# V's weights in five transfers between the first x tiles, later x loads by halves, and one SwiGLU product ahead of two normalisations

## The chip, the cores and the metric

The kernel runs on one core of one Trainium2 chip. The metric is device time in microseconds (us) of one execution, from the runtime's own measurement. A profiled execution gives, beside it, a span (from the first to the last instruction of the program) and a record of each instruction and each DMA transfer.

The engines are named as the profile names them: PE is TensorE (matrix products, with PEld its weight loads), DVE is VectorE, ACT is ScalarE, POOL is GpSimd, and SP is SyncE, which does no arithmetic here and issues the DMA transfers, one after another, in program order.

## The reference

The input x is one sequence of S = 2048 tokens of width D = 640. It is layer-normalised without weights, and the result xn feeds two branches whose outputs are added to x:

```
xn  = (x - mean(x)) / sqrt(var(x) + 1e-5)
out = x + A(xn) + B(xn)

A:  q, k, v = split(xn @ wqkv)                    # 32 heads of 20
    pq, pk  = q @ w_phi[h], k @ w_phi[h]          # per head
    phi(z)  = [softmax(z), softmax(-z)]           # 40 features per head
    kv = phi(pk)^T v ;  z = sum over tokens of phi(pk)
    o  = phi(pq) kv / (phi(pq) z + 1e-6)
    A  = o @ wo
B:  h = silu(xn @ w1) * (xn @ w3)                 # width F = 1536
    B = h @ w2
```

All weights and activations are bfloat16.

## The kernel before, in words

The 2048 tokens are 16 tiles of 128 tokens (t = 0 to 15); four tiles make a quarter of 512 tokens. The engines run the instructions in the order in which the function issues them (the block stands under a manual schedule), each engine and the SP queue in its own order; waits between them come from the data that they share. Eight DMA semaphores are used in turn: before it issues, a transfer also waits for the landing of the transfer eight places ahead of it.

The work falls into three stretches.

1. The start (lines 129 to 658). For each tile, `stats` (line 557) computes mean and variance on DVE (line 190, then 191) and a first 1/sqrt on POOL (lines 199 and 202); `lx` (line 564) refines it and writes the normalised tile in place (line 242, DVE; tiles 12 and 13 on ACT, line 237). `T` (`x_transposed`, line 247) turns the tile into xnT: tiles 0 to 7 by five 128 x 128 transposes on PE (line 262) that ACT copies out of PSUM (line 268), tiles 8 to 15 by a transposing DMA (line 251). `V` (`v_unit`, line 294) is the product of a tile with V's weights, ten matmuls (line 284), copied out by ACT (line 297). A `unit` is one block of 128 of the 1536 columns of SwiGLU for one quarter: ten matmuls into two PSUM banks, gp and up (line 381), and a tanh on ACT (line 389). Its product is issued later, by calling what `unit()` returned (g0 to g4): two instructions on DVE, gs (line 394) and h (line 397), which read gp and up and so free the two banks. There are six banks, used in turn; each `V` takes two as well. `FB` folds w_phi into K's weights (line 365).
2. Lines 661 to 674: for each tile the features of k (POOL normalises them, line 347), the sums kv, and SwiGLU units between them; then wo is loaded (line 673).
3. Lines 678 to 711: for each tile the features of q, the products with kv, and the output product of 34 matmuls (line 499) with the residual.

The loads at the start, all on the SP queue through `ld` (line 108), go in this order: x tiles 0 and 1 (160 KB each), all of V's weights (one transfer of 800 KB, lines 131 and 132), x tiles 2 and 3; then, held back by two one-element copies on ACT that write into their destinations (lines 587 and 590), the second quarter of x (640 KB in one transfer, `ld_x`, line 111), the first third of w1 and w3 (640 KB each), the third quarter of x, and w_phi. The fourth quarter of x reuses the room of the first, so it waits for the transposes of tiles 0 to 3. The x tiles lie in `xin`, a part of reg_h; V's weights, `wv`, lie in reg_w.

The order written out around the fifth unit, g4, is: phi_blocks() (one DVE instruction, line 356), the normalisation and transfer of tile 13, the matmuls of g4 (line 650), the normalisation of tiles 14 and 15 (`lx(14, 2)`), their transposing DMAs, `V(10)`, the product of g4 (line 654), `V(11)`, the loads of the last half of w1 and w3, the transposed load of Q's weights, and then `V(12)` with the first `FB`s.

Of the kernel before, what the change touches and what calls it, by code (L numbers as in the profile page):

```python
# [8 lines left out]
P = 128  # L9
# [3 lines left out]
def kernel(  # L13
# [24 lines left out]
    _, S, D = A_x.shape  # L38
    H, Dh = 32, 20
    F = B_w1.shape[1]  # L40
    NST, NSC, KD, KF = S // P, S // 512, D // P, F // P
# [19 lines left out]
    x2 = A_x[0]  # L61
# [11 lines left out]
    def pair(name):  # L73
# [18 lines left out]
    xin = reg_h[:, 8 * KF * P : 8 * KF * P + 3 * 4 * D].rearrange(  # L92
        "p (b t d) -> p b t d", b=3, t=4
    )
    w_nat = reg_w[:].rearrange("p (w c f) -> p w c f", w=3, c=KD)
    wkT, wqT, wv = w_nat[:, 0], w_nat[:, 1], w_nat[:, 2]
# [11 lines left out]
    def ld(dst, src):  # L108
        nc.sync.dma_start(out=dst, in_=src)

    def ld_x(q):
        ld(
            xin[:, q % 3],
            x2[q * 512 : (q + 1) * 512, :].rearrange("(t p) d -> p t d", p=P),
        )

    def w_of(i):
        return A_wqkv[:, i * D : (i + 1) * D].rearrange("(c p) f -> p c f", p=P)
# [6 lines left out]
    with tc.manual_schedule():  # L125
        def ldT(dst, i):
            nc.sync.dma_start_transpose(out=dst, in_=A_wqkv[:, i * D : (i + 1) * D])

        for t in range(4):
            ld(xin[:, 0, t], x2[t * P : (t + 1) * P, :])  # L130
            if t == 1:
                ld(wv, w_of(2))


        ident = one.tile([P, P], bf, name="ident")
# [68 lines left out]
        def ln_newton(t, n):  # L204


            r = slice(t, t + n)
            eng = nc.vector if t < BY_DMA else nc.gpsimd
            if n == 1:
                eng.tensor_scalar(  # L210
                    out=rstd[:, r], in0=ry[:, r], scalar1=ve[:, r], scalar2=ry[:, r],
                    op0=ALU.mult, op1=ALU.mult,
                )
            else:
                eng.tensor_mul(out=rstd[:, r], in0=ry[:, r], in1=ry[:, r])
                eng.tensor_mul(out=rstd[:, r], in0=rstd[:, r], in1=ve[:, r])
            if t < BY_DMA:
                nc.vector.scalar_tensor_tensor(
                    out=rstd[:, r], in0=rstd[:, r], scalar=-3.0, in1=ry[:, r],
                    op0=ALU.add, op1=ALU.mult,  # L220
                )
            else:
                nc.gpsimd.tensor_scalar(
                    out=rstd[:, r], in0=rstd[:, r], scalar1=-0.5, scalar2=1.5,
                    op0=ALU.mult, op1=ALU.add,
                )
                nc.gpsimd.tensor_mul(out=rstd[:, r], in0=rstd[:, r], in1=ry[:, r])
            if t in BY_ACT:
                nc.gpsimd.tensor_scalar(
                    out=shift[:, r], in0=mv[:, r, 0], scalar1=rstd[:, r], scalar2=-1.0,  # L230
                    op0=ALU.mult, op1=ALU.mult,
                )

        def ln_x(t):
            xt = xin[:, (t // 4) % 3, t % 4, :]
            if t in BY_ACT:
                nc.scalar.activation(
                    out=xt, in_=xt, func=AF.Identity,
                    scale=rstd[:, t : t + 1], bias=shift[:, t : t + 1],
                )  # L240
                return
            nc.vector.tensor_scalar(  # L242
                out=xt, in0=xt, scalar1=mv[:, t, 0:1], scalar2=rstd[:, t : t + 1],
                op0=ALU.subtract, op1=ALU.mult,
            )
# [130 lines left out]
        def glu_unit(sc, fi):  # L376

            gp, up = bank("gp"), bank("up")
            for ps, w in ((gp, w1), (up, w3)):
                for c in range(KD):  # L380
                    nc.tensor.matmul(  # L381
                        ps[:],
                        w[:, c, fi * P : (fi + 1) * P],
                        xnT[:, c, sc * 512 : (sc + 1) * 512],
                        start=(c == 0),
                        stop=(c == KD - 1),
                    )
            th = work.tile([P, 512], f32, name="th")
            nc.scalar.activation(out=th[:], in_=gp[:], func=AF.Tanh, scale=0.5)  # L389
            return lambda: glu_product(sc, fi, gp, up, th)  # L390
# [143 lines left out]
        def norm_unit(w, g, i):  # L534
            sq = work.tile([P, KD, 160], bf, name="sq")
            nc.scalar.activation(
                out=sq[:], in_=w[:, :, i * 160 : (i + 1) * 160],
                func=AF.Square, accum_out=norms[:, 4 * g + i : 4 * g + i + 1],
            )
# [24 lines left out]
        def lx(t0, n):  # L564
            if t0 < BY_DMA:
                ln_newton(t0, n)
            for t in range(t0, t0 + n):
                ln_x(t)
# [13 lines left out]
        def unit():  # L582
            return glu_unit(*glu.pop(0))


        stats(0, 1)
        nc.scalar.copy(out=xin[0:1, 1, 0, 0:1], in_=ry[0:1, 0:1])
        ld_x(1)
        stats(1, 1)
        nc.scalar.copy(out=w1[0:1, 0, 0:1], in_=ry[0:1, 1:2])  # L590
        ld_glu(0, 512)
        ld_x(2)
        ld(wps[:], A_w_phi.rearrange("h j f -> (h j) f").rearrange("(c p) f -> p c f", p=P))
        lx(0, 1)
# [10 lines left out]
        lx(3, 1)  # L605
        T(3)
        ld_x(3)
        ldT(wkT, 1)
        ld_glu(512, 768)
# [38 lines left out]
        lx(13, 1)  # L648
        T(13)
        g4 = unit()  # L650
        lx(14, 2)
        T(14, 15)
        V(10)
        g4()
        V(11)
        ld_glu(768, F)
        ldT(wqT, 0)
# [4 lines left out]
        for t in range(NST):  # L662
# [7 lines left out]
            fill(1)  # L670
            if t >= 12:
                norm_unit(wkphi, 0, t - 12)
        for k0, k1 in ((0, 3), (3, KD)):
            ld(wo[:, k0:k1], A_wo[k0 * P : k1 * P, :].rearrange("(c p) d -> p c d", p=P))


# [37 lines left out]
    with tc.If(ok == 0):  # L714
# [16 lines left out]
        with tc.For_i(0, NST, 1) as t:  # L731
# [5 lines left out]
            h = hT[:, bass.ds(t, 1)].rearrange("p a f s -> p (a f) s")  # L737
# [30 lines left out]
```

## Time and profile before

| | |
|---|---|
| median of three runs | 274.9 us (274.19 to 274.9) |
| the profiled execution's own time | 274.14 us |
| its span | 272.3 us |
| PE busy | 264.5 us (97% of the span) |
| DVE busy | 190.4 us (70%) |
| ACT busy | 111.8 us (41%) |
| POOL busy | 96.5 us (35%) |
| granted TensorE clock | 1.0 throughout |

The span leaves out 1.8 us of the execution's own time. The busy time of PE includes 60 matmuls on an identity matrix near the start whose results are not used (line 169), and the ends of matmuls are modelled, so that overlapping records can show as longer than the pace at which they follow each other. A few matmul records are missing: a group of five may show as four. In a timeline row the numbers are the start and the length in microseconds, the engine, the line, the operation, what it writes and reads, how many instructions were merged, and in brackets the idle time before the first and what ended it. For SPq rows the length is the time in which the queue issued, not the transfer.

### The profile page before, as it was taken

The page shows a single profiled execution, that of the slowest core. Times are in us where ns is not written, and L with a number is a line of the kernel's source. Part 1 is how long each engine was busy: PE and PEld are TensorE (multiplying, and loading weights), DVE is VectorE, ACT ScalarE, POOL GpSimd, SP SyncE. Part 2 cuts the span into 40 slices and gives each one's busy share as a digit, 9 for nine tenths or more (in the row PEclk, how much of TensorE's full clock was granted, in tenths as well). Part 3 has the DMA queues.
Part 4 walks back from the last instruction along what each step waited for, and adds up shares of the span by engine and source line. Part 5 has one row for each costly group of instructions (what it writes and reads, how often), then busy time and mean ns, then how long its engine had stood idle before and what let it go on. Part 6 is the DMA issues. An engine that isn't in the chain of part 4 may idle for free.

```text
span 272.3 us, 5207 instructions
## 1 busy us (share of the span) xinstructions
PE 264.5 (97%) x2000; PEld 167.8 (62%) x2018; DVE 190.4 (70%) x354; ACT 111.8 (41%) x262; POOL 96.5 (35%) x98
## 2 busy tenths in 40 slices
PE   7799999999999999999999999999999999999995
PEld 7557567555555555555554555677777777777773
DVE  5799850887766677777778778877776677777341
ACT  6656558543555554346555454522222222222000
POOL 5235730354433333344443312333333434433000
PEclk9999999999999999999999999999999999999999
DMA  7995459900000000000000974346665686556641
GB/s 206 337 256 147 79 94 314 218 0 2 0 0 2 0 2 0 1 4 0 0 2 0 278 119 77 77 112 133 144 141 130 130 129 144 127 130 148 145 103 54
DMA packets 60092, 27.14 MB, mean 100 GB/s; under 512 B 47136, under 2 KB 60064, under 8 KB 60064
## 3 DMA queue, kind: packets, MB, share of 16 engines
q1 hardware_dynamic: 60064, 26.77, 42.6%
q8 instruction: 17, 0.28, 0.4%
q14 instruction: 11, 0.09, 0.1%
HBM read 12.81 MB, written 2.62 MB: 57 GB/s over the span
## 4 chain that ended last, share of the span: by engine, by line
PE 90%; DVE 3%; DMA 2%; POOL 2%; issue 1%; SPq 0%; ACT 0%; DVEq 0%
PE acc L499 27%; PE up L381 18%; PE gp L381 18%; PE pq L284 8%; PE pk L284 8%; PE pv L284 5%; DMA reg_h<-in_A_x_dram 2%; PE pkv L407 2%; PE pr L436 2%; PE pf L365 1%; DVE st L190 1%; DVE reg_h L242 1%; POOL ry L202 1%; PE pst L262 1%; DVE reg_h L397 1%
## 5 line engine op out<-in xcount | busy, mean ns | idle before, releaser
L347 POOL TENSOR_TENSOR phi<-phi,rk 128x1320 bf16<-128x1320 bf16 x32 | 77.2, 2414 | 137.5 <-DVE rk L346 125.8
L344 DVE TENSOR_REDUCE sk<-phi 128x66 f32<-128x1320 bf16 x32 | 48.9, 1528 | 41.8 <-ACT phi L311 40.9
L381 PEld LDWEIGHTS <-w 128*128 128x128 bf16 x480 | 45.5, 98 | 50.2
L381 PE MATMUL up<-xnT,w 128*128 128x512 bf16 x237 | 59.5, 379 | 0.3
L381 PE MATMUL gp<-xnT,w 128*128 128x512 bf16 x225 | 58.5, 378 | 0.7
L284 PEld LDWEIGHTS <-xnT 128*128 128x128 bf16 x480 | 45.7, 97 | 21.7 <-issue 0.8
L499 PE MATMUL acc<-reg_v,reg_h 128*128 128x320 bf16 (+2 forms) x384 | 54.9, 299 | 0.0
L311 ACT ACTIVATE phi<-pq 128x360 bf16<-128x360 f32 (+1 forms) x64 | 23.3, 450 | 59.2 <-POOL phi L347 49.2
L499 PEld LDWEIGHTS <-reg_h 128*128 128x128 bf16 x384 | 37.3, 98 | 14.4
L389 ACT ACTIVATE th<-gp 128x512 f32<-128x512 f32 x48 | 28.8, 600 | 31.3 <-PE gp L381 27.2
L397 DVE SCALAR_TENSOR_TENSOR reg_h<-gs,up 128x512 bf16<-128x512 bf16 x48 | 33.0, 687 | 4.9
L311 ACT ACTIVATE phi<-pk 128x360 bf16<-128x360 f32 (+1 forms) x64 | 23.3, 451 | 24.7 <-PE pk L284 15.7
L394 DVE SCALAR_TENSOR_TENSOR gs<-th,gp 128x512 bf16<-128x512 f32 x48 | 31.5, 656 | 0.5 <-ACT th L389 0.5
L508 DVE TENSOR_TENSOR res<-acc,xr 128x320 bf16<-128x320 f32 (+2 forms) x32 | 14.3, 486 | 21.2 <-PE acc L499 21.2
L284 PE MATMUL pk<-wkphi,xnT 128*128 128x360 bf16 (+2 forms) x160 | 24.6, 300 | 0.0
L284 PE MATMUL pq<-wqphi,xnT 128*128 128x360 bf16 (+2 forms) x160 | 24.6, 299 | 0.0
L499 PE MATMUL acc<-reg_w,reg_v 128*128 128x320 bf16 (+2 forms) x160 | 24.5, 299 | 0.0
L284 PE MATMUL pv<-reg_w,xnT 128*128 128x320 bf16 x160 | 23.5, 299 | 0.4 <-DVE reg_h L397 0.3
L346 DVE RECIPROCAL rk<-sk 128x66 f32<-128x66 f32 x32 | 18.1, 566 | 3.2
L499 PEld LDWEIGHTS <-reg_v 128*128 128x128 bf16 x160 | 15.7, 98 | 6.1
L190 DVE BATCH_NORM_STATS2 st<-reg_h 128x6 f32<-128x320 bf16 x32 | 13.7, 471 | 4.2 <-DMA reg_h<-in_A_x_dram 4.2
L297 ACT CAST reg_v<-pv 128x320 bf16<-128x320 f32 x32 | 12.1, 431 | 10.9 <-PE pv L284 10.9
(63 smaller groups left out, 140.2 us busy)
## 6 DMA issues: line engine op xcount, KB each, us to landing
xr<-in_A_x_dram SPq DMA_DIRECT2D x16, 160.0 KB, 2.5
out_dram<-res SPq DMA_DIRECT2D x15, 160.0 KB, 1.8
reg_h<-in_A_x_dram SPq DMA_DIRECT2D x3, 640.0 KB, 5.9
w<-in_B_w_dram SPq DMA_DIRECT2D x2, 960.0 KB, 6.4
reg_v<-in_B_w_dram SPq DMA_DIRECT2D x4, 480.0 KB, 5.3
w<-in_B_w_dram SPq DMA_DIRECT2D x2, 640.0 KB, 7.3
reg_w<-in_A_wqkv_dram SPq DMA_DIRECT2D x1, 800.0 KB, 6.1
reg_h<-in_A_x_dram SPq DMA_DIRECT2D x4, 160.0 KB, 4.1
```

The costliest lines, as they stand in the source:

```text
L190: nc.vector.bn_stats(out=st[:, i, :], in_=xt[:, i * HD : (i + 1) * HD])
L284: nc.tensor.matmul(ps[i][:, 0 : b - a], xnT[:, c, cols], w[:, c, a:b], start=(c == 0), stop=(c == KD - 1), skip_group_check=True,)
L311: nc.scalar.activation(out=to[g], in_=p.rearrange("p (c f) -> p c f", f=60), func=AF.Exp, scale=1.0 - 2.0 * g,)
L344: nc.vector.reduce_sum(out=sk[:], in_=rows, axis=AX.X)
L346: nc.vector.reciprocal(out=rk[:], in_=sk[:])
L347: nc.gpsimd.tensor_mul(out=rows, in0=rows, in1=rk[:, :, :, None].to_broadcast([P, 2 * NCH, 3, Dh]))
L381: nc.tensor.matmul(ps[:], w[:, c, fi * P : (fi + 1) * P], xnT[:, c, sc * 512 : (sc + 1) * 512], start=(c == 0), stop=(c == KD - 1),)
L389: nc.scalar.activation(out=th[:], in_=gp[:], func=AF.Tanh, scale=0.5)
L394: nc.vector.scalar_tensor_tensor(out=gs[:], in0=th[:], scalar=1.0, in1=gp[:], op0=ALU.add, op1=ALU.mult)
L397: nc.vector.scalar_tensor_tensor(out=hT[:, 4 * sc : 4 * sc + 4, fi, :], in0=gs[:].rearrange("p (t s) -> p t s", t=4), scalar=0.5, in1=up[: ...
L499: nc.tensor.matmul(ps[:, 0 : b - a], rows[j][0], rows[j][1][:, a:b], start=(j == 0), stop=(j == len(rows) - 1),)
L508: nc.vector.tensor_tensor(out=res[:, a:b], in0=ps[:, 0 : b - a], in1=xr[:, a:b], op=ALU.add)
```

## The change

Four edits:

- V's weights are loaded in five transfers of 128 rows (160 KB each): three between x tiles 1 and 2, two between x tiles 2 and 3.
- `ld_x`, which loads the later quarters of x, issues two transfers of two tiles instead of one of four.
- The product of g4 is issued before the normalisation of tiles 14 and 15 instead of after `V(10)`.
- wo is loaded in three transfers (2, 2 and 1 blocks of 128 rows) instead of two (3 and 2).

```diff
     def ld_x(q):
-        ld(
-            xin[:, q % 3],
-            x2[q * 512 : (q + 1) * 512, :].rearrange("(t p) d -> p t d", p=P),
-        )
+        for h in range(2):
+            ld(
+                xin[:, q % 3, 2 * h : 2 * h + 2],
+                x2[q * 512 + h * 256 : q * 512 + h * 256 + 256, :].rearrange(
+                    "(t p) d -> p t d", p=P
+                ),
+            )
...
-        for t in range(4):
+        for t, chunks in ((0, ()), (1, (0, 1, 2)), (2, (3, 4)), (3, ())):
             ld(xin[:, 0, t], x2[t * P : (t + 1) * P, :])
-            if t == 1:
-                ld(wv, w_of(2))
+            for c in chunks:
+                ld(wv[:, c], A_wqkv[c * P : (c + 1) * P, 2 * D : 3 * D])
...
         lx(13, 1)
         T(13)
         g4 = unit()
+        g4()
         lx(14, 2)
         T(14, 15)
         V(10)
-        g4()
         V(11)
...
-        for k0, k1 in ((0, 3), (3, KD)):
+        for k0, k1 in ((0, 2), (2, 4), (4, KD)):
             ld(wo[:, k0:k1], A_wo[k0 * P : k1 * P, :].rearrange("(c p) d -> p c d", p=P))
```

The numbers of arithmetic instructions stay as they are; the SP queue issues eight transfers more (four for V's weights, three for x, one for wo), and no more bytes. Each of the five matmul pairs of `V(0)` now waits for its own block of V's weights, where before the first waited for all.

## The prediction

> **What bounds the kernel now.** I read the page first (busy shares and the chain that ended last), then PE's waits, then the chain in order of time, and last the timeline of the places where the chain leaves PE.
>
> ```profile
> span 272.3 us, 5207 instructions
> PE 264.5 (97%) x2000; PEld 167.8 (62%) x2018; DVE 190.4 (70%) x354; ACT 111.8 (41%) x262; POOL 96.5 (35%) x98
> ...
> PE 90%; DVE 3%; DMA 2%; POOL 2%; issue 1%; SPq 0%; ACT 0%; DVEq 0%
> ```
> ```profile
> PE pst L262 <- DVE reg_h L242: 1.8, 4, 0.7
> PE pv L284 <- DVE reg_h L397: 0.3, 1, 0.3
> ```
> ```profile
> 2.19 6.05 DMA reg_h<-in_A_x_dram
> 27.57 0.61 ACT th L389
> 38.82 1.38 PE pv L284 x9
> 45.85 1.38 PE pk L284 x10
> ```
>
> PE is the bound: nine tenths of the chain are its own work. After 45.85 us the chain stays on PE up to the last residual, so a microsecond taken from PE's start is one taken from the end. What PE waits for, its second view says: 1.8 us for normalised tiles before the transposes of tiles 0 to 3, and 0.3 us once for a SwiGLU product (a bank to come free). The chain names the load behind it: x tile 2, issued at 2.19, lands 6.05 us later, at 8.24, and DVE starts its statistics at 8.27. The other stretch in which the chain is off PE, 27.57 to 38.82, runs over DVE and POOL to the second wait.
>
> The first stretch:
>
> ```profile
> 0.80 0.87 SPq L109 DMA_DIRECT2D reg_h<-in_A_x_dram  x2
> 1.72 0.43 SPq L109 DMA_DIRECT2D reg_w<-in_A_wqkv_dram  x1
> 2.75 0.43 SPq L109 DMA_DIRECT2D reg_h<-in_A_x_dram  x1
> 6.75 0.45 DVE L242 TENSOR_SCALAR reg_h<-reg_h,mv,rstd 128x640 bf16<-128x640 bf16 x1
> 7.26 0.45 PE L262 MATMUL pst<-ident,reg_h 128*128 128x128 bf16 x5 [0.34 <-DVE reg_h L242]
> 7.83 2.88 PE L284 MATMUL pv<-reg_w,xnT 128*128 128x320 bf16 x20
> 8.27 0.89 DVE L190 BATCH_NORM_STATS2 st<-reg_h 128x6 f32<-128x320 bf16 x2 [1.06 <-DMA reg_h<-in_A_x_dram]
> 9.31 0.83 DVE L190 BATCH_NORM_STATS2 st<-reg_h 128x6 f32<-128x320 bf16 x2
> 10.61 0.76 ACT L297 CAST reg_v<-pv 128x320 bf16<-128x320 f32 x2 [0.60 <-PE pv L284]
> 11.40 0.45 PE L262 MATMUL pst<-ident,reg_h 128*128 128x128 bf16 x5 [0.69 <-DVE reg_h L242]
> 11.92 0.45 DVE L242 TENSOR_SCALAR reg_h<-reg_h,mv,rstd 128x640 bf16<-128x640 bf16 x1
> 12.28 0.88 DVE L190 BATCH_NORM_STATS2 st<-reg_h 128x6 f32<-128x320 bf16 x2
> 12.42 0.45 PE L262 MATMUL pst<-ident,reg_h 128*128 128x128 bf16 x5 [0.57 <-DVE reg_h L242]
> 12.71 2.88 PE L284 MATMUL pv<-reg_w,xnT 128*128 128x320 bf16 x20
> ```
>
> DVE has nothing to do from 7.20 (6.75 + 0.45) to 8.27: 1.07 us, and it is waiting for x tile 2. From 8.27 it works without a stop to be seen here: tile 3 is normalised at 12.37, its transposes start at 12.42, `V(2)` at 12.71. After that PE is on the chain until 27.57.
>
> **Edit 1, V's weights in five.** Nothing changes for tiles 0 and 1. The queue issues a load every 0.46 us (0.80 to 1.72 is two). Tile 2 becomes its sixth load and is issued at 0.80 + 5 x 0.46 = 3.10 (was 2.19); tile 3 the ninth, at 4.48 (was 2.75). But ahead of tile 2 lie only two tiles and three blocks, 5 x 160 KB, instead of seven times 160 KB. When do they land?
>
> ```profile
> reg_h<-in_A_x_dram SPq DMA_DIRECT2D x1, 160.0 KB, 2.3
> reg_h<-in_A_x_dram SPq DMA_DIRECT2D x1, 160.0 KB, 5.9
> reg_w<-in_A_wqkv_dram SPq DMA_DIRECT2D x1, 800.0 KB, 6.1
> 0.00:5.70 5.70, 4.28 (x54) 4.28 (x54) 2.48 (x8) 3.94 (x3) 3.56 (x22) 1.00 0.63 175
> 0.00:7.20 7.20, 5.28 (x65) 4.94 (x65) 3.80 (x12) 4.61 (x6) 4.08 (x22) 1.00 0.72 205
> 3.20:4.20 1.00, 1.00 (x13) 1.00 (x11) 0.97 (x4) 1.00 (x1) 0.27 (x4) 1.00 0.75 119
> ```
>
> The first three rows are issues and their time to landing: tile 1 (issued at 1.26, landed at 3.6), tile 3 (2.75 to 8.65), V's weights (1.72 to 7.8). The others end in the rate of the DMA engines in GB/s. The bounds of the time to landing are thus 2.3 and 6.1 us: tile 2 between 5.4 and 9.2, tile 3 between 6.8 and 10.4 (by its own row, 5.9). I take values from the bytes. A transfer of 160 KB is 164 kB. By 5.70 the engines had moved 175 x 5.70 = 998 kB, six transfers (983); by 7.20, 205 x 7.20 = 1476 kB, all nine. The completion adds 0.4 (tile 1: two transfers, 328 kB, were through at about 3.2, by the same count, and it landed at 3.6). So tile 2 at 6.1 and tile 3 at 7.6. That is near the lower bound, since between 3.20 and 4.20, behind tile 1 and at the start of the 800 KB transfer, the rate falls to 119 GB/s, against 205 on average; small transfers may not have that dip, which I don't count.
>
> Both are in time: DVE is free for tile 2 at 7.20 and for tile 3 1.04 later (9.31 - 8.27), at 8.24. So the whole of DVE's sequence moves from 8.27 to about 7.23, by 1.04. What is late next? Tile 3's transposes come at 12.42 - 1.04 = 11.38. `V(0)` and `V(1)` stand before them on PE: `V(0)` starts at 7.83, just after V's weights land (1.72 + 6.1 = 7.8); with its first block there, it follows tile 1's transposes as `V(2)` follows tile 3's, 12.71 - 12.42 = 0.29 after them, at 7.55, and `V(1)` ends at 10.43 instead of 10.71. ACT's copies of `V(1)` end at 11.09 (10.61 + 0.76 - 0.28), and it can then copy tile 2's transposes, in two instructions of 0.385, so that `V(2)` has its first half of xnT at 11.48. It starts at 11.67: 1.04 gained. If `V(0)` doesn't start earlier, the same path gives 11.76 and about 0.9. The blocks of V's weights are wanted at 7.55 and every 0.27 us after that (two matmuls of 2.88 / 20); the last, the eighth transfer, by the bytes is there before 7.6, against 8.6. The four added waits on PE I cost at nothing; the 0.95 us between 10.43 and 11.38 covers them, and without cover ACT's copies pass them on one for one.
>
> **Edit 2, later x by halves.** Three more issues of about 0.4 us on SP. The second quarter:
>
> ```profile
> 5.45 0.38 SPq L109 DMA_DIRECT2D reg_h<-in_A_x_dram  x1
> reg_h<-in_A_x_dram SPq DMA_DIRECT2D x1, 640.0 KB, 5.8
> w<-in_B_w_dram SPq DMA_DIRECT2D x1, 640.0 KB, 8.0
> 6.47 0.95 SPq L109 DMA_DIRECT2D w<-in_B_w_dram  x2
> 16.50 1.24 PE L381 MATMUL up<-xnT,w 128*128 128x512 bf16 x5
> ```
>
> It lands whole at 11.2 now, and DVE will want tile 4 at 12.28 - 1.04 = 11.24; the whole load would just do, half of it is there sooner. The second half is issued at 5.9 and finished at 6.3, before the queue's next wait ends at 6.47, so w1 and w3 keep their places. w3, the second of the two issued from 6.47 on, leaves at about 6.9 and lands 8.0 later, at 14.9; `up` will want it at 16.50 - 1.04 = 15.46: cover 0.6. If it came later than that, the excess would be lost on PE. The third and fourth quarters are used long after they land. Cost 0.
>
> **Edit 3, g4 earlier.**
>
> ```profile
> 34.68 0.98 DVE L356 TENSOR_TENSOR wphi<-wps,mask 128x800 bf16<-128x800 bf16 x1
> 36.58 0.80 DVE L242 TENSOR_SCALAR reg_h<-reg_h,mv,rstd 128x640 bf16<-128x640 bf16 x2 [0.92 <-POOL rstd L227]
> 38.08 0.69 DVE L397 SCALAR_TENSOR_TENSOR reg_h<-gs,up 128x512 bf16<-128x512 bf16 x1
> 38.82 1.38 PE L284 MATMUL pv<-reg_w,xnT 128*128 128x320 bf16 x9 [0.32 <-DVE reg_h L397]
> 44.33 1.52 PE L284 MATMUL pv<-reg_w,xnT 128*128 128x320 bf16 x10
> ```
>
> DVE idles 0.92 us ahead of the two normalisations, for POOL. The product, from 37.30 to 38.77, can start at 35.66 and ends about 37.1, so PE finds its bank free and the 0.32 us go. The normalisations then start at 37.1 instead of 36.58, 0.5 later; tiles 14 and 15 are sent and loads of w1 and w3 issued 0.5 later behind them. Tile 15's products at 44.33 come more than three microseconds after its transposing DMA lands (about 41), which covers 0.5 + 0.3. Gain 0.32.
>
> **Edit 4, wo in three.** One more issue; wo is used only by the output products, over 100 us later. 0.
>
> **Sum.** 1.04 + 0.32 = 1.36. The profiled execution took 274.14 (span 272.3 and 1.8 around it): 272.8. That is just under the lowest of the three runs (274.19); their median is 0.76 higher, so I give 274.9 - 1.4 = **273.5**. A change under 0.3% (0.8 us) can't be told from none here.
>
> **Rivals.** (a) Tile 3 lands no sooner than now, at 8.65: it left last then and leaves last now. Only 0.6 of the 1.04 is won (9.31 - 8.68, the start of its statistics now and then), with 0.32 total 0.9: 274.0. For it: the bytes were through at 7.2 and tile 3 still landed 1.4 later, so some DMA engine lagged. (b) The stretch behind absorbs the shift: w3 or a copy on ACT is late by most of a microsecond, and only edit 3 shows: 274.6, no change. Against it: DVE, POOL and ACT there start from tile 3 and move with it. (c) Slower: tile 3, issued 1.73 later, again needs 5.9 us and lands at 10.4. DVE then reaches it 1.1 later than now (10.4 against 9.31), and the sum is +1.1 - 0.3 = 275.7. It decides from a landing at 9.6 on. For it: its row; against it: the same bytes are ahead of it as now. (d) Transfers follow each other instead of overlapping: nine of 2.3 put tile 3 at 21.5, 12 us late, 287. Against it: tiles 0 and 1 were issued 0.46 apart, and DVE's first statistics (3.09) and the landing of tile 1 (3.6) are 0.5 apart. The Trainium skill speaks for (d) in part: "DMA: Bandwidth & Descriptors", section "Rules for kernel authors", says that many small transfers should be coalesced into one, and the section "Anatomy of one DMA" puts a fixed cost of about 2.0 us on each (fitted on GpSimd's path, this queue is SP's); by that four added transfers would cost 8 us if the fixed parts added up. The trace has 2.3 for a lone 160 KB and shows these parts overlapping, and the same page's table of rules says the fixed cost overlaps when a transfer is issued early.
>
> **How the numbers follow.** The forecast 0.58 (its own range 272.6 to 274.0), (a) 0.14, (b) 0.10, (c) 0.15, (d) 0.01, the rest 0.02. The range: below, the dip of 3.20 to 4.20 gone and the lower runs as the base, 272.3; above, up to the middle part of (c), 275.4. Faster: the forecast and half of (a), 0.66; same: the other half and (b), 0.16; slower: (c), (d) and the rest, 0.18.
>
> **What would show it.** Right: in the profile after, x tile 2 and 3 landing before 7.2 and 8.2, no DMA wait ahead of line 190 but the first, `V(2)` at about 11.7, no wait of PE for line 397, the first `pk` at about 44.5 instead of 45.85, span near 270.9. Wrong: a wait of line 190 for tile 3, a wait in `V(0)` for a block, a new wait of `up` for w3, or a first `pk` that has moved and an end that hasn't.

## The result, and the profile after

The changed kernel takes 273.19 us (median of 22 runs, 272.42 to 274.48) against 274.37 us for the kernel before on the same chip (22 runs, 273.0 to 275.39). The ratio is 0.9967, with a 95% interval of 0.9952 to 0.9981: faster by 0.9 us, between 0.5 and 1.3 (the means of the runs are 0.9 us apart, their medians 1.2). The forecast was 1.4 us faster, 273.5 us, so the way was right and the time lies in the range, but only two thirds of the gain came. One execution of the kernel called e4 below took 469.4 us at a granted clock of 0.66 and is left out of its ratio.

The profiled execution is less kind: 273.94 us of its own time, 272.1 of span, where the span before was 272.3. Its page (busy times, and the shares of the chain that ended last), then its list of what PE waited for (total, times, longest):

```profile
span 272.1 us, 5238 instructions
PE 266.4 (98%) x2018; PEld 169.1 (62%) x2018; DVE 190.3 (70%) x354; ACT 111.3 (41%) x262; POOL 96.2 (35%) x98
PE 93%; DMA 4%; DVE 1%; POOL 0%; issue 0%; SPq 0%; ACT 0%
PE idle L173 <- POOL ident masks.py:199: 1.4, 1, 1.4
PE up L385 <- DMA w<-in_B_w_dram: 0.8, 1, 0.8
PE pst L266 <- DVE reg_h L246: 0.3, 1, 0.3
```

The 1.8 us of waits for normalised tiles have become 0.3, and the wait for g4's bank is gone. Not all of that is gain: the warm-up matmuls (line 173 here) ended at 7.34 us, where they had ended at 6.03, so the waits for tiles 0 and 1 (0.21 and 0.34 us before) are now filled with matmuls whose results are not used. In place of the waits stands a wait of 0.8 us of `up` for a load, which is w3. The timeline shows where the microsecond was won and where it went (line numbers are four higher than before from line 133 on):

```profile
1.42 5.92 PE L173 MATMUL idle<-ident 128*128 128x128 bf16 x56 [1.42 <-POOL ident masks.py:199]
7.18 0.44 PE L266 MATMUL pst<-ident,reg_h 128*128 128x128 bf16 x5
7.19 0.88 DVE L194 BATCH_NORM_STATS2 st<-reg_h 128x6 f32<-128x320 bf16 x2
8.10 2.89 PE L288 MATMUL pv<-reg_w,xnT 128*128 128x320 bf16 x20
8.41 0.89 DVE L194 BATCH_NORM_STATS2 st<-reg_h 128x6 f32<-128x320 bf16 x2
11.52 0.45 PE L266 MATMUL pst<-ident,reg_h 128*128 128x128 bf16 x5 [0.26 <-DVE reg_h L246]
11.99 2.89 PE L288 MATMUL pv<-reg_w,xnT 128*128 128x320 bf16 x20
14.71 1.24 PE L385 MATMUL gp<-xnT,w 128*128 128x512 bf16 x5
16.75 1.25 PE L385 MATMUL up<-xnT,w 128*128 128x512 bf16 x5 [0.80 <-DMA w<-in_B_w_dram]
45.47 1.54 PE L288 MATMUL pk<-wkphi,xnT 128*128 128x360 bf16 x10
```

DVE goes on to tile 2 without a stop, at 7.19 instead of 8.27. `V(2)` starts 0.72 us sooner (11.99 against 12.71), `gp` of g0 0.71 sooner. Then `up`, at 16.75, is 0.25 us later than before (16.50). From there PE works through; with g4's wait gone the first `pk` in the timeline is at 45.47, against 45.69 before, and the end follows it. In this execution the 0.7 us won at the start were lost again on w3, and what is left is close to edit 3 alone.

The loads themselves: issue groups with size and time to landing, of tile 2 (issued at 3.13), tile 3 (4.56) and w3 (7.00), and the stretch from 4 to 10 us, whose last number is the rate of the DMA engines in GB/s.

```profile
reg_h<-in_A_x_dram SPq DMA_DIRECT2D x1, 160.0 KB, 3.9
reg_h<-in_A_x_dram SPq DMA_DIRECT2D x1, 160.0 KB, 3.8
w<-in_B_w_dram SPq DMA_DIRECT2D x1, 640.0 KB, 9.7
4.00:10.00 6.00, 6.00 (x62) 5.34 (x61) 5.46 (x20) 2.84 (x9) 2.73 (x8) 1.00 0.90 268
```

The same stretch before:

```profile
4.00:10.00 6.00, 5.33 (x65) 4.25 (x63) 4.62 (x15) 3.23 (x9) 2.08 (x6) 1.00 1.01 334
```

Tile 2 lands at about 7.1 and tile 3 at 8.4, in time or nearly so, but between 4 and 10 us the DMA engines move 268 GB/s instead of 334. Over six microseconds that is 0.4 MB less (66 x 6). Up to 4 us they moved more than before, 138 GB/s against 106, so that at 10 us about 0.27 MB are missing, 0.8 us of transfer at 334. w3, further back in the queue, lands at 16.7 instead of 14.9.

The lower rate alone is not what PE waited for, however. Each of these transfers leaves sixteen landing records in the trace, and the landing times here are those of the last. Of w3's, fifteen are in by 15.09 (before: 14.85), and the sixteenth follows at 16.71 (before: 14.86). `up` could have started at 15.95 (16.75 - 0.80), so the whole wait is for the last sixteenth.

### The profile page after: what moved, and what is told of

Its sections match the earlier page's. It is cut to its first block, busy times and chain, and to the rows that moved or that the text cites. A ratio compares the mean times of both kernels' runs of the same rounds, so it can differ in the third digit from the quotient of the medians.

```text
span 272.1 us, 5238 instructions
## 1 busy us (share of the span) xinstructions
PE 266.4 (98%) x2018; PEld 169.1 (62%) x2018; DVE 190.3 (70%) x354; ACT 111.3 (41%) x262; POOL 96.2 (35%) x98
## 4 chain that ended last, share of the span: by engine, by line
PE 93%; DMA 4%; DVE 1%; POOL 0%; issue 0%; SPq 0%; ACT 0%
PE acc L503 27%; PE up L385 19%; PE gp L385 19%; PE pq L288 8%; PE pk L288 8%; PE pv L288 6%; DMA w<-in_B_w_dram 4%; PE pkv L411 2%; PE pr L440 2%; PE pf L369 1%; DMA reg_h<-in_A_x_dram 1%; DVE st L194 1%; PE pst L266 0%; POOL ry L206 0%; DVE mv L195 0%
## 5 line engine op out<-in xcount | busy, mean ns | idle before, releaser
L385 PE MATMUL gp<-xnT,w 128*128 128x512 bf16 x240 | 59.6, 378 | 0.0
L194 DVE BATCH_NORM_STATS2 st<-reg_h 128x6 f32<-128x320 bf16 x32 | 13.8, 473 | 3.3 <-DMA reg_h<-in_A_x_dram 3.2
```

Source lines behind the costliest of these rows:

```text
L194: nc.vector.bn_stats(out=st[:, i, :], in_=xt[:, i * HD : (i + 1) * HD])
L385: nc.tensor.matmul(ps[:], w[:, c, fi * P : (fi + 1) * P], xnT[:, c, sc * 512 : (sc + 1) * 512], start=(c == 0), stop=(c == KD - 1),)
```

## The experiments

Times are ratios to the kernel before on the same chip. The columns "tile 2, tile 3" and "w3" are landing times (us), worked out from the trace as issue plus time to landing; "rate" is the DMA rate from 4 to 10 us; "first pk" is its start in the timeline. Each profile is one execution.

| kernel | V's weights | x halves | g4 early | ratio (95% interval) | tile 2, tile 3 | rate | w3 | PE waits for w3 | first pk |
|---|---|---|---|---|---|---|---|---|---|
| before | one | no | no | 1 | 8.2, 8.7 | 334 | 14.9 | 0 | 45.69 |
| changed | five | yes | yes | 0.9967 (0.9952 to 0.9981) | 7.1, 8.4 | 268 | 16.7 | 0.8 | 45.47 |
| e1 | five | no | no | 0.9995 (0.9976 to 1.0015) | 6.5, 8.3 | 265 | 15.3 | 0 | 44.70 |
| e2 | one | yes | no | 0.9998 (0.9976 to 1.0020) | 8.0, 8.4 | 342 | 15.1 | 0 | 45.41 |
| e3 | one | no | yes | 0.9975 (0.9955 to 0.9996) | 8.4, 8.8 | 327 | 15.0 | 0 | 45.36 |
| e4 | five | no | yes | 0.9978 (0.9956 to 1.0000) | 6.6, 8.1 | 265 | 15.1 | 0 | 44.41 |
| e5 (wo in two) | five | yes | yes | 0.9974 (0.9964 to 0.9985) | 6.8, 8.3 | 261 | 16.3 | 0.6 | 45.03 |
| e6 (w1, w3 in halves) | five | yes | yes | 0.9969 (0.9958 to 0.9981) | 6.6, 8.1 | 284 | 14.5, 16.5 | 0 | 44.87 |
| e7 | two | yes | yes | 0.9964 (0.9950 to 0.9978) | 7.3, 8.6 | 331 | 15.0 | 0 | 44.58 |
| e8 | five | yes | no | 0.9983 (0.9963 to 1.0002) | 7.3, 8.5 | 266 | 16.6 | 0.7 | 45.80 |
| e9 | two | no | no | 0.9982 (0.9966 to 0.9997) | 6.4, 7.7 | 336 | 13.7 | 0 | 44.57 |
| e10 | two | no | yes | 0.9963 (0.9943 to 0.9984) | 6.9, 8.2 | 334 | 13.8 | 0 | 44.68 |
| e11 (48 warm-ups) | two | no | yes | 0.9998 (0.9980 to 1.0017) | 6.3, 7.6 | 327 | 15.3 | 0 | 44.12 |
| e12 (48 warm-ups) | one | no | no | 1.0022 (1.0002 to 1.0043) | 7.7, 8.1 | 333 | 14.7 | 0 | 45.15 |

In e8 the first of the ten records of that `pk` is missing; it began about 0.1 us sooner.

### One edit at a time: e1, e2, e3

My theory after the result was that the loss on w3 comes from the five small transfers ("blocks"); the rival was that the halves of x cause it ("halves"). e1, e2 and e3 are the kernel before with edit 1, 2 or 3 alone, as the diff of the change has it.

> Edit 1 alone: V's weights in five transfers, everything else as before. Theory 'blocks' (many small transfers lower the DMA rate of the first 12 us, so w3 lands at 16 to 17 and PE waits for it): DVE's statistics of tile 2 start near 7.2 and V(2) near 12.0, but PE waits 0.5 to 1 us for w3, so the first pk comes at about 45.6 to 45.9 and the time is 0 to 0.4 us under before. Rival 'halves' (the three extra x transfers make w3 late): w3 lands by 15.2, no wait of PE for it, and the whole 0.8 to 1.0 us is won.

> Edit 2 alone: later x loads by halves, V's weights in one transfer. 'Blocks': w3 lands about where it does now (14.9, within 0.5), time unchanged within 0.3 us. 'Halves': w3 lands at 16 to 17; up wants it at 16.5, so the time is 0 to 0.5 us above before.

> Edit 3 alone: g4's product ahead of the normalisation of tiles 14 and 15. Both theories: the 0.3 us wait of PE for line 397 is gone, the first pk 0.3 us sooner, time 0.3 us under before, which the interval may not tell from none. If the runs of the changed kernel gained their 0.9 us here alone, this shows 0.9.

PE's waits from 12 us on, in e1:

```profile
PE pv L284 <- DVE reg_h L397: 0.3, 1, 0.3
```

Its DMA rate from 4 to 10 us:

```profile
4.00:10.00 6.00, 6.00 (x65) 5.25 (x64) 5.55 (x20) 3.13 (x9) 2.84 (x8) 1.00 0.89 265
```

and in e2, with V's weights whole and x by halves:

```profile
4.00:10.00 6.00, 6.00 (x64) 5.29 (x63) 4.87 (x16) 3.02 (x9) 2.36 (x6) 1.00 1.02 342
```

The five transfers lower the rate (265 against 334 and 342), as "blocks" had it. But w3 is in time in e1, so they don't make it late by themselves, and e2 shows that the halves don't either. Both theories missed. In e1's profile edit 1 wins its whole 1.0 us (first `pk` at 44.70); its runs, 0.1 us faster with an interval of 0.7 faster to 0.4 slower, don't bear that out, and their interval leaves out the forecast 1.04. e2 shows no change (0.7 us faster to 0.5 slower), as the prediction said. In e3 the wait for g4's bank is gone; PE's waits from 12 us on are

```profile
PE pst L262 <- DVE reg_h L242: 0.6, 1, 0.6
```

and the first `pk` is 0.33 us sooner. Its runs give 0.7 us, with an interval (0.1 to 1.2) that holds the 0.3.

### Together: e4, e5, e8

e4 leaves edit 2 out, e5 edit 4, e8 edit 3; the rest of the change stays.

> Edits 1, 3 and 4, with the later x loads whole as before. 'Blocks': w3 still lands after 16 and PE waits 0.4 to 1 us for it; time as the changed kernel, 0.5 to 1.0 us under before. 'Halves': no wait for w3, 1.2 to 1.4 us under before. If tile 4's statistics wait for the whole load (landing after 11.4), DVE idles there and part of the gain of edit 1 goes.

> The changed kernel with wo in two transfers as before (edits 1, 2 and 3): undoes edit 4 and gives a second profile of a start that is the same as the changed kernel's. If edit 4 is worth nothing, time as the changed kernel, 0.5 to 1.3 us under before. 'Together' (the five blocks and the halves together make w3 late, since each alone did not): w3 lands after 15.8 again and PE waits 0.3 to 1 us. 'Chance' (the late w3 was one execution's): w3 lands by 15.4, no wait, first pk near 44.4.

> The changed kernel without edit 3 (g4's product after V(10) as before): its distance to the changed kernel is edit 3's worth in place. By the profiles: the wait of PE for g4's bank near 38 is back (0.3 us), w3 lands after 16 and PE waits 0.6 to 0.8 us for it, so 0 to 0.4 us under before. If edit 3 carries most of the gain in the runs (it alone gave 0.7, edit 1 alone 0.1), this is within 0.3 us of before; if edit 1 carries it, 0.6 us under.

PE's wait for w3 is back wherever the blocks and the halves stand together; in e5:

```profile
PE up L384 <- DMA w<-in_B_w_dram: 0.6, 1, 0.6
```

and in e8, where g4's wait is back as well:

```profile
PE up L384 <- DMA w<-in_B_w_dram: 0.7, 1, 0.7
PE pv L287 <- DVE reg_h L400: 0.3, 1, 0.3
```

Of the profiles with both edits and w3 whole, three of three have w3 at 16.3 to 16.7 and a wait of 0.6 to 0.8; with the blocks alone (e1, e4) w3 lands at 15.1 to 15.3, with the halves alone (e2) at 15.1, and nobody waits. So the late w3 isn't one execution's chance alone, and "blocks" failed again in e4.

The landing records show the same in all three: fifteen of w3's sixteen are in by 15.64 in e5 and by 15.34 in e8, before `up` wants them (15.69 and 15.91), and the last comes at 16.27 and 16.55. In e1, e2 and e4 the last two lie within 0.3 us of each other. But a last record that lags isn't peculiar to the two edits: in the kernel before, fifteen parts of the second quarter of x were in by 9.92 and the last at 11.20, and in e11 and e12, below, w3's last part came 0.8 us after the fifteenth. That it takes both edits to put such a lag on w3 is thus likely and not shown. Its cause stays open; the trace doesn't tell which DMA engine was last. Each profile has one 16 KB packet on the instruction queue, 1.0 to 1.3 us long, that starts between 12.6 and 14.8; whether it holds up the last part was not tested.

No effect of edit 4 shows (0.9974 against 0.9967, intervals overlapping).

### Around the wait: e6 and e7

e6 lets `up` wait for half as much; e7 keeps the change but makes V's weights two transfers.

```diff
-        ld_glu(0, 512)
+        ld_glu(0, 256)
+        ld_glu(256, 512)
```

> The changed kernel, with the first third of w1 and w3 loaded in two column halves each (256 columns of both, then the next 256), so that the first up has to wait for half as much. If w3 is what takes the gain back, the first half of w3 lands near 13.5, PE waits nowhere between 12 and 45, the first pk comes near 44.3, and the time is 1.2 to 1.5 us under before. If the runs lose elsewhere, the time stays at 0.9 under before or less though the wait is gone. If two more transfers slow the DMA engines further, x tiles 4 to 7 are late and DVE waits.

```diff
-        for t, chunks in ((0, ()), (1, (0, 1, 2)), (2, (3, 4)), (3, ())):
+        for t, cut in ((0, None), (1, (0, 3)), (2, (3, KD)), (3, None)):
             ld(xin[:, 0, t], x2[t * P : (t + 1) * P, :])
-            for c in chunks:
-                ld(wv[:, c], A_wqkv[c * P : (c + 1) * P, 2 * D : 3 * D])
+            if cut:
+                ld(wv[:, cut[0] : cut[1]], w_of(2)[:, cut[0] : cut[1]])
```

> The changed kernel with V's weights in two transfers (three blocks, then two) at the same places, so six issues stand before tile 3's end instead of nine. 'Blocks' (many small transfers lower the DMA rate): the rate between 4 and 10 us is back near 330 to 350 GB/s, tile 2 still lands before 7.2, w3 before 15.3, no wait of PE for it, time 1.0 to 1.4 us under before. If the number of transfers doesn't matter, the rate stays at 270 and w3 is late as in the changed kernel.

e7's rate from 4 to 10 us, and the row of its first `pk`:

```profile
4.00:10.00 6.00, 6.00 (x62) 5.36 (x61) 5.32 (x18) 2.76 (x9) 2.59 (x7) 1.00 1.00 331
44.58 1.54 PE L287 MATMUL pk<-wkphi,xnT 128*128 128x360 bf16 x10
```

In e7 the rate is back and w3 is in time, as expected: it is five transfers of 160 KB that cost rate, and two of 480 and 320 KB don't. First `pk` is 0.9 us sooner than in the changed kernel's profile. In e6 the wait is gone too, but the first `pk` gains only 0.6 on the changed kernel. The runs don't follow: 0.8 us faster than before for e6 and 1.0 for e7, which can't be told from the changed kernel's 0.9. In the changed kernel's unprofiled executions the wait for w3 must therefore cost less than in its profile, or something else in e6 and e7 must take it back; that was not settled.

### Fewest transfers: e9 and e10

Both are made from the kernel before with V's weights in two as in e7; e10 has g4 early as well.

> Only V's weights, in two transfers (three blocks, two blocks) at the places of edit 1; x whole, g4 as before. If the DMA rate is what keeps edit 1 alone from showing in the runs, this form keeps 330 GB/s between 4 and 10 us, has no wait for w3, and is 0.7 to 1.0 us under before, in the runs as in the profile. If freeing DVE early isn't worth what the profile says, it is within 0.3 us of before.

> V's weights in two transfers and g4's product early, x and wo as before: the version with the fewest transfers. If the two gains add and the halves of x are worth nothing, 1.0 to 1.4 us under before and not behind the changed kernel. If tile 4's statistics wait for the whole second quarter of x (landing after 11.4), DVE idles there and the gain falls under 1.0.

e9 is 0.5 us faster than before (0.1 to 0.9), e10 1.0 us (0.4 to 1.6). As far as the intervals tell, the two gains add (0.5, and 0.7 in e3), and no use of the halves of x shows: in e9 and e10 the second quarter lands whole at 9.8 and 10.0, and tile 4's statistics start at 11.2. e10 is at least as good as the changed kernel with seven transfers fewer; the intervals don't part the two.

e10 also shows what is late next. Its rows around `V(0)`:

```profile
7.36 0.44 PE L262 MATMUL pst<-ident,reg_h 128*128 128x128 bf16 x5
7.86 0.44 PE L262 MATMUL pst<-ident,reg_h 128*128 128x128 bf16 x5
8.28 2.89 PE L284 MATMUL pv<-reg_w,xnT 128*128 128x320 bf16 x20
12.17 1.12 PE L284 MATMUL pv<-reg_w,xnT 128*128 128x320 bf16 x7 [0.34 <-ACT xnT L268]
```

Tile 0's transposes start at 7.36, not at 6.24, though DVE had normalised it at 6.16: PE is still in the warm-up matmuls. `V(0)` follows at 8.28, and `V(2)` waits for ACT's copies, which the late `V(1)` holds back.

### The warm-up: e11 and e12

Of the twelve profiles up to e10, eleven have a median record of 311 to 314 ns for these matmuls, and only that of the kernel before has 219. In it the pace nearly doubles at about 4.2 us: a matmul starts every 107 ns until then and every 56 ns after it. In seven of the others this change comes at 4.9 to 6.7 us, and in four, the changed kernel among them, not within the 56. The count of the warm-up matmuls by microsecond, before:

```profile
3.50:4.50 1.00, 1.00 (x15) 1.00 0.78 187
4.50:5.50 1.00, 1.00 (x22) 1.00 1.07 374
```

and in the changed kernel:

```profile
3.50:4.50 1.00, 1.00 (x13) 1.00 0.84 246
4.50:5.50 1.00, 1.00 (x12) 1.00 0.86 266
```

All 56 took 4.61 us there and 5.92 here, with the granted clock at 1.00 in both. The Trainium skill names this: "TensorE: Matmul & The Clock Gate", "Part 1: The HAM clock gate", says that the array runs at half rate until it has been busy for one window of about 3.4 us, and that the window runs freely, so that the moment depends on where in it the first matmul falls. The profiles agree in kind, but the spread is wider than the 500 ns to either side that the page gives: the 56 ended 4.6 to 6.1 us after they began. In the kernel before the pace changed 2.8 us after the first matmul, sooner than one such window, and in four profiles more than 5.6 us after it.

e11 is e10, and e12 the kernel before, with

```diff
-    WARM = 56
+    WARM = 48
```

> V's weights in two transfers, g4 early, and 48 warm-up matmuls instead of 56. In twelve profiles the 56 took 4.6 to 6.1 us; from about 5.5 on they hold up tile 0's transposes and V(0). Theory 'warm-up is next': they end 0.6 to 0.9 us sooner, V(0) starts by 7.7 in any execution, V(2) by 11.7, no wait of PE for ACT near 12, and the time is 1.2 to 1.5 us under before (0.2 to 0.4 under the same kernel with 56). Rival 'warm-up is needed': the first V products run at the slow pace (20 matmuls take 4 to 5 us instead of 2.9) and the time is 1 us or more over that of 56. If neither, no difference.

> The kernel before with 48 warm-up matmuls, nothing else. There V(0) waits for V's weights (7.8) and the statistics of tile 2 for its load (8.2), so the end of the warm-up has 0.7 us of room behind V(1): 'warm-up is next' expects no change, within 0.3 us. A gain of more would say that the warm-up held up the kernel already before the change.

The profile of e11 is the best of all: span 271.0, first `pk` at

```profile
44.12 1.54 PE L284 MATMUL pk<-wkphi,xnT 128*128 128x360 bf16 x10
```

Its runs say otherwise: 0.9998, no faster than before, where e10, on another chip, had 0.9963. And e12 is 0.6 us slower than before (0.1 to 1.2). My theory falls: a shorter warm-up lost in the runs in both kernels. The rival is that real work then runs at the slow pace. e12's profile shows the beginning of that, in the transposes of tile 0,

```profile
6.51 0.74 PE L262 MATMUL pst<-ident,reg_h 128*128 128x128 bf16 x5
```

which took 0.45 us before. But tile 1's transposes start only 0.1 us later than before, and `V(0)` takes 2.88 and 2.89 us in the two profiles, so the rival is argued and not shown as the cause of the loss. For e11 there is another, also untested: w3 landed at 15.3 and `up` started at 15.41, so that a start this early leaves w3 hardly any cover. e12's profile has a further delay, its last output transfer: time to landing of its 64 KB,

```profile
out_dram<-res SPq DMA_DIRECT2D x1, 64.0 KB, 3.0
```

against, before,

```profile
out_dram<-res SPq DMA_DIRECT2D x1, 64.0 KB, 1.6
```

and the end waits for it.

## Why the prediction was right or wrong

**DVE freed 1.04 us sooner: right in this profile.** The statistics of tile 2 start at 7.19 (forecast 7.23), of tile 3 at 8.41 (8.24). The landings were forecast too early, 6.1 and 7.6 against 7.1 and 8.4. The count of bytes held up to 5.70 us (177 GB/s from the start, against 175 before) and was 0.1 MB short at 7.20 (191 against 205). What failed is the 0.4 us from the bytes to the landing: of tile 2's sixteen landing records the eighth stands at 6.05 and the last at 7.06. Tile 2 was still in time; tile 3 cost 0.2. The 1.04 itself comes from one landing of tile 2, at 8.24. In the four profiles with V's weights in one transfer it landed at 7.7 to 8.4, so DVE's idle time there was between 0.5 and 1.2 us.

**`V(0)` at 7.55, `V(2)` at 11.67: late by 0.55 and 0.3.** They came at 8.10 and 11.99. The step took tile 1's transposes, and with them the end of the warm-up, from one execution, and that end was the earliest of twelve. The path by ACT's copies that the prediction gave for a `V(0)` at 7.83 fits: with 0.27 us more it gives 12.03. Of the 1.04 us, 0.72 reached `V(2)`.

**w3's cover of 0.6 us: this is the step that failed in the profile.** The prediction held w3 at 14.9 because its issue kept its place (it did, 7.00 against 6.9). Its landing didn't: 9.7 us after issue instead of 8.0, 1.8 late, and PE waited 0.8, for the last sixteenth of it. The sum had 0 for edit 2 and no delay of later loads for edit 1; in the profile the two together took back all that edit 1 had won. It is rival (b) in that execution, by the mechanism that it named. That w3 took the gain back in the runs too isn't shown: e1 has no such wait and gained 0.1 us in its runs, and e6 and e7, without the wait, gained no more than the changed kernel. What cost edit 1 its gain in the runs stays open.

**g4 earlier, 0.32: right** in size in the profile of e3 and in the changed kernel, where the wait for line 397 is gone; in the runs the changed kernel is 0.0016 ahead of e8, 0.4 us, which the intervals don't tell from none.

**Edit 4, nothing: right** as far as e5 tells.

**The sum, 1.36 against 0.9 (0.5 to 1.3): right in sign, too large.** With edit 3 at 0.3 to 0.4, edit 1 with its loss is left with about half a microsecond instead of 1.04. The runs of e1 (0.1 us) and e3 (0.7) put more of the gain on edit 3; their intervals don't settle the split. The averaged profiles lie on the side of edit 1 being worth less than 1.04: with 0.32 taken off where g4 is late, the first `pk` is at 45.27 in the mean of the three with V's weights whole (before, e2, e3), 44.94 in the six with five transfers (0.3 sooner) and 44.50 in the three with two and 56 warm-ups (0.8 sooner). `V(2)` starts at 12.67, 11.89 and 11.94 in the means of the same groups, so that five pieces win as much as two up to there and lose part of it behind. That the time came so near the forecast is in part luck: the base, the median of three runs, was 274.9, and 22 runs gave 274.37, so a base 0.5 too high met a gain 0.5 too large. (By their own terms the chances of faster and same add up to 0.65 and 0.17, not 0.66 and 0.16.) The rivals (a), (c) and (d) didn't come: tile 3 landed 0.3 us sooner than before, not later, and nine transfers overlapped. But the Trainium skill's rule beside (d), to coalesce small transfers ("DMA: Bandwidth & Descriptors", "Rules for kernel authors"), did hold as a loss of rate, which neither the forecast nor (d) had priced: 265 GB/s from 4 to 10 us with five transfers of 160 KB (e1), 331 to 336 with two. Over the first 10 us the difference is smaller, 210 to 227 against 242 to 249.

## What to carry to other kernels

When a load is moved ahead by cutting another into pieces, look at the cover of the last load queued behind the pieces, not only of the first, and allow for its last part to land a microsecond or more after the rest. Here two pieces gave the early tile at the old rate, and five took a fifth of the rate from 4 to 10 us away. The runs favour two over five in all three pairs (changed and e7, e1 and e9, e4 and e10), by 0.1 to 0.4 us, but in none beyond the intervals. A place that waits has often hidden something else that varies from one execution to the next: before a step forward is counted, see by how much the neighbouring row moves between profiles. Gains under a microsecond are judged by the runs: among these kernels the best single profile belonged to one that was no faster.

## What was not expected of the hardware

- Five transfers of 160 KB for one of 800 KB lowered the mean DMA rate from 4 to 10 us to 261 to 268 GB/s in five profiles (284 in e6), against 327 to 342 with one or two. Up to 4 us the five moved more, 134 to 149 GB/s against 104 to 119.
- The last of a transfer's sixteen landing records can come long after the fifteenth: 0.6 to 1.6 us for w3 in the three profiles with five pieces and halves, 1.3 us for the second quarter of x in the kernel before, and 0.0 to 0.3 us for w3 in e1, e2, e4 and the kernel before.
- The pace of the first matmuls nearly doubled, from one in 107 ns to one in 56, anywhere between about 4.2 us after the start of the span and after all 56 had run, while the granted clock in the profile stood at 1.00; the same 56 took 4.61 to 6.10 us.
- The time of the last 64 KB store from issue to landing was 1.5 to 2.1 us in most profiles and 3.0 in one, and the end waits for it.
